# Side matmuls behind PV, the fourth output tile kept in the side bank, an earlier last FFN and a new tile table, in a planned attention + FFN kernel

## The chip, the cores and the metric

One core of a Trainium2 chip. The metric is the device time of one execution in microseconds. A span is shorter than the device time by some 1.8 us: it runs from the first to the last recorded instruction. Three things are called by short names throughout: the **side bank** is PSUM bank 7, the **tail** is what follows the end of the last exponential, **excess** is the time by which an exponential or a tanh ends later after its predecessor than the undisturbed distance of its kind.

## The reference, cut to what matters

```python
x = A_x                                  # 2048 x 512, bf16
xn = layernorm(x)
q = xn @ wq  (32 heads of 16);  k = xn @ wk;  v = xn @ wv      # one K and V for all heads
A = concat_heads(softmax(q k^T / 4) v) @ wo
B = gelu(xn @ w1 + b1) @ w2 + b2         # 512 -> 1792 -> 512, tanh form
return x + A + B
```

## The kernel before

Scores are computed in tiles of 128 keys x 512 queries of one head, 2048 tiles, three to a **unit** (683 units). A unit's three tiles stand in three PSUM banks, and the next unit's in three others. ScalarE takes exp of two or three of them in one instruction. Where the table `DTAB` says `0` or `2`, that tile of the unit goes to VectorE (DVE) instead, which builds an approximate exp from five integer images of the score; PV then takes five matmuls for the tile instead of one. So each such letter takes work from ScalarE (0.427 us, the distance between exponentials of three and of two tiles in the trace) and gives it to DVE (0.68 us for the first piece and a third of 0.548 us for each of the four others) and PE.

```python
# exp(u): ScalarE's share of unit u; the tiles named by DTAB go to p1
exps.append(act(lambda e: e.activation(E[:, s0:s0 + na, :], bank(b0, na)..., ACT.Exp, scale=LN2 / 128.0), ...))
for i, t in enumerate(ts):
    if is_d[t]:
        p1(t, 3 * x + i)                   # DVE reads the score bank
# close_batch: four more images of up to three such tiles, then five PV matmuls for each
```

PE does score matmuls (three side by side in rows of the array), and "column" matmuls of 128x32 weights, four side by side: PV in bank 6, whose sum is called O, and all else, called side matmuls, in the side bank: next queries (`q`), the FFN's first layer (`h`), and the output tiles (`y`: 14 FFN pieces, `wo`: 8 head groups, for each 128 rows). In the trace of the kernel before, the three score matmuls start together and take 0.39 us; the first column matmul starts 0.32 us behind them, and then four start every 0.22 us, each taking 0.38. So the first comes some 0.1 us later than in the rhythm of the fours (an estimate from 0.32 and 0.22). The block of 512 queries is done in 170.75 units; its output tiles are made during the next block, and those of the last block as early as its FFN allows.

The order in each engine's queue is fixed when the kernel is built. The source gives each operation a duration and an `allow`, called its lateness below. A list schedule takes, of what is ready in the plan, the operation with the smallest `rdy + allow`, where `rdy` is the time at which its inputs are ready in the plan (or with the smallest `due`, where one is set). A side operation also has a release: the unit after whose exponential it may be planned at the earliest. The queues run in that order where the chip's durations differ from the plan's too: in the run below that puts side matmuls ahead of PV again, two of DVE's first pieces start only behind an add that stands before them and waits 0.74 us for PE.

```python
return (o.rdy + o.allow if o.due is None else o.due), o.idx         # the key: smallest first

def act(fn, r=(), w=(), n=TBW, allow=0.0, **kw):
    return add("act", fn, r, w, occ=0.051 + n / 1.2e3, lat=0.22, allow=allow, **kw)
def mm4(o, l, rh, start, stop, r=(), w=(), allow=1.5, **ak):        # side matmuls: four columns
    ...
def pv_mm(gg, j, v, kt, rhs, r):
    add("pe", ..., allow=4.0 if gg < NTB * NGR - 1 or kt < NT - 4 else -5.0, kind="pv", tag=(gg, j))

def y_tile(tb, i):                        # last block: FFN part and FIN_G=5 head groups, put by
    y_mm(tb, i, fts=range(FT - FIN_F))
    wo_mm(tb, i, range(FIN_G))
    dve(lambda e: e.tensor_tensor(xpy[:, i, :], pM, x_sb[:, ti, :], ALU.add), ...)     # + residual

FB = (2, 3, 4, 5)                         # the other groups, in score banks that come free at the end
for i in range(4): wo_mm(tb, i, range(FIN_G, NGR - 1), start=True, stop=False, bk=FB[i])
for i in range(4): mm4(bank(FB[i]), oT[last group], wop[:, NGR - 1, :], False, True, ...)
for i in range(4):
    dve(lambda e, i=i, ti=ti: e.tensor_tensor(x_sb[:, ti, :], bank(FB[i]), xpy[:, i, :], ALU.add), ...)
    store(tb, i)
```

Note that PV of the last head group is urgent (-5) only for its last four key tiles; before that a PV matmul (4.0) stands behind a side matmul (1.5) that became ready at the same time.

## Time and profile before

| | before |
|---|---|
| median of 3 runs, before the prediction | 814.35 us (814.28 to 814.74) |
| span of the profiled run, granted clock | 812.5 us, 0.985 |
| busy share of PE, DVE, ScalarE | 96%, 91%, 96% |
| exponentials of three and of two tiles | 265 and 418 |
| end of the last exponential | 799.5 us |
| side matmuls still to do then | 99 by start time |

How to read it: three engines are above 90%, so the shares decide nothing. The chain of waits names ScalarE for 82% of the span; its exponentials stand end to end. What can be won without taking work from ScalarE is the excess between them and the tail. The lines for both stand in the prediction.

### The profile page before, as it was taken

Reading aid. Unit: us, or ns where it says so; the run is one execution under the profiler, and the core shown is the slowest. Engines: PE = TensorE matmul, PEld = TensorE weight load, DVE = VectorE, ACT = ScalarE, POOL = GpSimd, SP = SyncE. Lnnn points to the kernel's source line nnn. Section 1 sums busy time; section 2 is a strip of 40 time slices with the busy share of each in tenths; the row PEclk is TensorE's granted clock in tenths of the full one; section 3 lists DMA queues with packets and bytes.
Section 4 is the critical chain, followed back from the end, with each engine's and each line's share of the span. In section 5 each row is a group of like instructions: output and inputs, shape, how many; then the busy total and the mean of one; then the engine's idle time right before and its main releaser. Section 6 shows DMA issues by size and latency. Waiting matters only on the chain.

```text
span 812.5 us, 21402 instructions
## 1 busy us (share of the span) xinstructions
PE 779.8 (96%) x9184; PEld 240.4 (30%) x9186; DVE 742.5 (91%) x1424; ACT 783.5 (96%) x733; POOL 23.7 (3%) x79
## 2 busy tenths in 40 slices
PE   6799999999999999999999999999999999999998
PEld 4332222222222223222322223322222222322233
DVE  7499999999997898999998769999998898999986
ACT  4899999999999999999999999999999999999993
POOL 6500000000000000000000000000000000000000
PEclk7799999999999999999999999999999999999999
DMA  9000000000000000000000000000000000000000
GB/s 308 13 22 16 16 15 7 23 3 16 15 15 22 28 10 16 15 16 16 15 15 12 19 23 23 15 15 4 16 15 22 22 23 21 10 8 15 16 15 27
DMA packets 23976, 19.09 MB, mean 24 GB/s; under 512 B 12369, under 2 KB 19402, under 8 KB 23882
## 3 DMA queue, kind: packets, MB, share of 16 engines
q1 hardware_dynamic: 22298, 17.17, 7.2%
q8 instruction: 73, 1.20, 0.6%
q10 hardware_dynamic: 1584, 0.56, 0.3%
q14 instruction: 21, 0.17, 0.1%
HBM read 14.98 MB, written 2.35 MB: 21 GB/s over the span
## 4 chain that ended last, share of the span: by engine, by line
ACT 82%; PE 15%; DMA 1%; POOL 1%; DVE 1%; issue 0%; ACTq 0%; POOLq 0%
ACT E L855 78%; PE pAll L551 5%; PE pAll L876 5%; PE pAll L836 4%; ACT ub L978 3%; DMA ub<-in_A_wq_dram 1%; PE pAll L545 1%; ACT ub L675 0%; ACT xnT L693 0%; DVE x_sb L1131 0%; POOL V L794 0%; PE pAll L688 0%; POOL wqp L797 0%; ACT KT L707 0%; ACTq L558 0%
## 5 line engine op out<-in xcount | busy, mean ns | idle before, releaser
L855 ACT ACTIVATE E<-pAll 128x1024 bf16<-128x1024 f32 (+1 forms) x683 | 746.1, 1380 | 3.6 <-PE pAll L836 3.3
L876 PE MATMUL pAll<-Dt,V 128*32 128x512 bf16 x2085 | 349.7, 383 | 0.5
L872 DVE TENSOR_SCALAR Dt<-pAll 128x512 int16<-128x512 f32 x417 | 280.1, 681 | 39.4 <-PE pAll L836 38.4
L876 PE MATMUL pAll<-E,V 128*32 128x512 bf16 x1631 | 301.9, 387 | 1.2 <-DVE Of L900 1.1
L887 DVE TENSOR_SCALAR Dt<-Dt 128x1536 int16<-128x1536 int16 (+2 forms) x600 | 286.1, 519 | 1.0 <-PE pAll L876 0.2
L836 PE MATMUL pAll<-QT,KT 32*128 32x512 bf16 x2048 | 269.1, 387 | 15.5 <-ACT E L855 8.3
L836 PEld LDWEIGHTS pAll<-QT,KT 32*128 32x128 bf16 x2048 | 68.6, 91 | 304.5 <-ACT E L855 247.9
L876 PEld LDWEIGHTS pAll<-Dt,V 128*32 128x32 bf16 x2085 | 94.3, 95 | 87.8 <-issue 45.1
L551 PE MATMUL pAll<-w_sb,ub 128*32 128x512 bf16 x896 | 109.2, 383 | 0.0
L876 PEld LDWEIGHTS pAll<-E,V 128*32 128x32 bf16 x1631 | 73.8, 94 | 61.4 <-issue 44.6
L551 PE MATMUL pAll<-wop,oT 128*32 128x512 bf16 x512 | 81.8, 382 | 0.0
L551 PE MATMUL pAll<-xnT,w_sb 128*32 128x512 bf16 x896 | 80.0, 384 | 1.1 <-DVE hb L964 0.6
L551 PE MATMUL pAll<-xnT,wqp 128*32 128x512 bf16 x496 | 45.1, 398 | 0.5 <-POOL wqp L797 0.3
L1139 PE MATMUL pAll<-xnT,zeros 128*32 128x512 bf16 x396 | 44.1, 384 | 0.0
L964 DVE TENSOR_SCALAR hb<-pAll,b1T 128x512 bf16<-128x512 f32 x56 | 41.2, 735 | 0.0
L551 PEld LDWEIGHTS pAll<-w_sb,ub 128*32 128x32 bf16 x896 | 29.0, 95 | 21.4 <-issue 14.7
L978 ACT ACTIVATE ub<-ub 128x1536 bf16<-128x1536 bf16 (+1 forms) x20 | 31.5, 1576 | 0.0
L730 DVE CAST QT<-pAll 128x512 bf16<-128x512 f32 x32 | 21.7, 680 | 9.8 <-PE pAll L551 7.7
L551 PEld LDWEIGHTS pAll<-xnT,w_sb 128*32 128x32 bf16 x896 | 21.0, 95 | 29.7 <-issue 16.8
L551 PEld LDWEIGHTS pAll<-wop,oT 128*32 128x32 bf16 x512 | 22.3, 95 | 13.6 <-issue 8.5
L900 DVE COPY Of<-pAll 128x512 f32<-128x512 f32 x31 | 21.0, 679 | 0.7 <-PE pAll L876 0.6
L911 DVE TENSOR_TENSOR oT<-Of,rbc 128x512 bf16<-128x512 f32 x31 | 21.1, 679 | 0.0
(109 smaller groups left out, 264.5 us busy)
## 6 DMA issues: line engine op xcount, KB each, us to landing
rbc<-rden_rows SPq DMA_DIRECT2D x124, 64.0 KB, 2.0
w_sb<-in_B_w_dram SPq DMA_DIRECT2D x2, 1792.0 KB, 13.0
x_sb<-in_A_x_dram SPq DMA_DIRECT2D x8, 256.0 KB, 6.9
out_dram<-x_sb SPq DMA_DIRECT2D x16, 128.0 KB, 1.7
QT<-mT SPq DMA_DIRECT2D x60, 2.0 KB
ub<-in_A_wq_dram ACTq DMA_DIRECT2D x1, 512.0 KB, 7.7
wop<-in_A_wo_dram SPq DMA_DIRECT2D x4, 128.0 KB, 2.7
den<-Of SPq DMA_DIRECT2D x31, 8.0 KB
```

Source lines behind the costliest of these rows:

```text
L551: add("pe", lambda e, c=c, j=j: e.matmul(o[c, :], l[:, c], rh, start=start, stop=stop, tile_position=(0, 32 * j)), r, [(k, j) for k in w] ...
L730: dve(lambda e: e.tensor_copy(QT[:, hq, :], bank(bk)), w=[B(bk)] + [(B(bk), j) for j in range(4)] + [("QT", hq)] + [("QTm", hq, j) for j i ...
L836: ins = e.matmul(o, l, rh, start=True, stop=True, tile_position=(q0, 0))
L855: exps.append(act(lambda e: e.activation(E[:, s0:s0 + na, :], bank(b0, na).rearrange("p (a n) -> p a n", a=na), ACT.Exp, scale=LN2 / 128.0 ...
L872: dve(lambda e: e.tensor_scalar(Dt[:, KZ, s, :], bank(bk), float(127 * 128) + SPL_D, SPL_MIN, ALU.add, ALU.max), w=[B(bk), ("D", s, KZ)], ...
L876: add("pe", lambda e, a, b: e.matmul(pO[32 * j:32 * j + 32, :], V1[:, v, kt, :], rhs, start=a, stop=b, tile_position=(0, 32 * j)), r=r + [ ...
L887: dve(lambda e, k=k: e.tensor_scalar(Dt[:, k, s0:s0 + n, :], Dt[:, KZ, s0:s0 + n, :], float(SPL_K[k]), None, ALU.add), r=[("D", s0 + i, KZ ...
L900: dve(lambda e: e.tensor_copy(Of[:, i, :], pO), w=["O", ("Of", i)], allow=0.0)
L911: onorm[gg] = dve(lambda e: e.tensor_tensor(oT[:, gg % NOT, :], Of[:, i, :], rbc[:, i, :], ALU.mult), r=[("Of", i)] + [("rbc", i, j) for j ...
L964: dve(lambda e: e.tensor_scalar(hb[:, ft % 6, :], pM, b1T[:, ft:ft + 1], None, ALU.add), r=["b1T"], w=M4 + [("h", ft % 6)], allow=ev)
L978: act(lambda e: e.activation(uu, uu, ACT.Tanh, scale=GELU_K), r=uk, w=uk, n=c, allow=al - 0.5, kind="tanh")
L1139: pr.filler = lambda e, j, o: e.matmul((pO if o else pM)[32 * j:32 * j + 32, :], zeros[:, 0:32], xnT[:, 0, 0:TBW], start=not o, stop=not o ...
```

## The change

It wants PE's order at the end to put attention first, the tail to lose its DVE adds, and the FFN of the last block to be out of the way earlier; a new table goes with it. The core of the diff (cut: the two tables of 683 letters, new names for values that stay as they were, the plumbing that hands `al` through, and one `due=0.0`, by which the output matmuls of the last head group go to the front of PE's queue once they are ready):

```diff
-LB = 120                       # last block: FFN spread over units LA to LB
-LY = 5                         # output tiles released LY units apart
-LS = 122                       # from unit LS
-FIN_G = 5
+LB = 105
+LY = 9
+LS = 107
+FIN_G = 4
-DTAB = "....2.0202..022.22...2222..."      # 417 tiles on DVE: 124 letters 0, 293 letters 2
+DTAB = "....2.2020.202.2.2...22.2022..."    # 414 tiles on DVE: 148 letters 0, 266 letters 2
+Y_ALLOW = 8.0                  # allow of the output tiles of earlier blocks (was 1.5)
+H_ALLOW = 5.0                  # of the FFN's first layer, earlier blocks alone (was 1.5)
+YT_ALLOW = (3,3,3,3)           # of the last block's output tiles (was 1.5)
+S_LAT = 0.27                   # planned latency of scores (was 0.22)
...
         def y_tile(tb, i):
-            y_mm(tb, i, fts=range(FT - FIN_F))
-            wo_mm(tb, i, range(FIN_G))
-            dve(... xpy = pM + x_sb ...)
+            y_mm(tb, i, al=YT_ALLOW[i])
+            wo_mm(tb, i, range(FIN_G), stop=i < 3, al=YT_ALLOW[i])
+            if i < 3:
+                dve(... xpy = pM + x_sb ...)
+            else:
+                mm4(pM, ident, x_sb[:, ti, :], False, False, ..., allow=YT_ALLOW[i])
...
-        FB = (2, 3, 4, 5)
+        FB = (2, 3, 4, 7)
...
-        for i in range(4):  dve(add of bank FB[i] and xpy); store
+        for i in (0, 1, 3, 2):
+            if i < 3:  dve(add of bank FB[i] and xpy)
+            else:      act(lambda e: e.activation(x_sb[:, ti, :], bank(FB[i]), ACT.Copy))
+            store(tb, i)
```

More of the change, by code (lines that the diff above doesn't have):

```diff
@@ L50 @@
 TBL = 1
-DTAB = "....2.0202..022.22...2222.2022...222.20....002.20.22.202.222....22222.0.020.22.022...2022200...02.0200.0..222..22.000.2202200...2020.2.0.22.0002.2...22222...222.2222.00..2222.2.2022020.202....2.02022.02.22..02....22020..0.222202.0.0..222.2220..22.02020......0..20...22.2222......02200..22.22.2020...2.2222.2.0..22.220...22022.0.0202.222.2...22222.222.20.22220....222020.2.2222.2.2....220.20.0.2202.2......202.2.0..220.0..200.....02..0..222.22.20....222.0.22020.222.0...22.22222.0..2.2220...2.20222..02.22.2020...22222.22.202..2.22...2.22020.22.202.2220..2220.0000.222.22.20...00.22..20.202.02.2....2.0.2.2.2.2.20202...2.20.2.2.2.2.22..20...0202.22.202.02002....22220222.2022.20.20..."
+DTAB = "....2.2020.202.2.2...22.202222..2022.20...2..2..20220.0.2222....2020.20.0202.0.002...2022.200...2.2000.0..220.2.2.0.202002020....002.2.22.0.2002.2...2.222002..02220.02...202.222202.02.2222....022222.202022..222...22200.00.0222.2022...2.20..22.2.2.20.20.....2020..2.22002020....20.22..020.222....0..22.0..2222.0...0220...20.00.0220.2200.22...22222.02.220.22220...2.22020.202202.022....2020.000.2200.2.0....202.2.2..220.0..2.0...0....2.0.2...22.00.....02220.2.222020.0....2.220.20...222222...2.22022.0022.2.2200....2222.22.202..2.22...2.220202.202.2202.0..2220.0000.222.220.....20.22.2200020..02....2..0...22...2.020.0....020202....2.02.20...2022.22.220.02022....22200222.2.2..202.0..."
+Y_ALLOW = 8.0
+H_ALLOW = 5.0
+YT_ALLOW = (3,3,3,3)
+WF_ALLOW = 1.5
+QP_ALLOW = 1.5
+S_LAT = 0.27
+YS = 9
+HA = 40
+HB = 165
 KM_DUE = 5.0
@@ L837, in fn @@
                 return ins
-            return add("pe", fn, r, [B(3 * x + i) for i in range(len(ts))], occ=0.216, lat=0.22, allow=-1.0, kind="S")
+            return add("pe", fn, r, [B(3 * x + i) for i in range(len(ts))], occ=0.216, lat=S_LAT, allow=-1.0, kind="S")
         eptr = [0]
@@ L943, in q_group @@
             for hq in hqs:
-                q_proj(tb, hq, 7, mm4)
+                q_proj(tb, hq, 7, mm4, allow=QP_ALLOW)
                 q_evac(tb, hq, 7, allow=EV_ALLOW)
@@ L962, in h_mm @@
                 mm4(pM, w1_sb[:, d, ft * P:(ft + 1) * P], xnT[:, d, tb * TBW:(tb + 1) * TBW], d == 0, d == DT - 1,
-                   r=["w1"] + tr(4 * tb, 4 * tb + 4), w=[B(7)])
+                   r=["w1"] + tr(4 * tb, 4 * tb + 4), w=[B(7)], allow=H_ALLOW if tb < NTB - 1 else 1.5)
             dve(lambda e: e.tensor_scalar(hb[:, ft % 6, :], pM, b1T[:, ft:ft + 1], None, ALU.add),
@@ L980, in h_chain, with y_mm, wo_mm @@
             dve(lambda e: e.tensor_tensor(uu, uu, hh, ALU.mult), r=uk + hk, w=uk, n=c, mode=2, allow=al)
-        def y_mm(tb, i, start=True, stop=False, bk=7, fts=range(FT)):
+        def y_mm(tb, i, start=True, stop=False, bk=7, fts=range(FT), al=1.5):
             for ft in fts:
                 mm4(bank(bk), ub[:, ft, i * P:(i + 1) * P], w2_sb[:, ft, :], start and ft == fts[0], stop and ft == fts[-1],
-                   r=[("u", ft), "w2"], w=[B(bk)])
-        def wo_mm(tb, i, gs, start=False, stop=True, bk=7):
+                   r=[("u", ft), "w2"], w=[B(bk)], allow=al)
+        def wo_mm(tb, i, gs, start=False, stop=True, bk=7, al=1.5):
             for n, g in enumerate(gs):
@@ L990, in wo_mm @@
                 mm4(bank(bk), oT[:, (tb * NGR + g) % NOT, i * P:(i + 1) * P], wop[:, g, :], start and n == 0,
-                   stop and n == len(gs) - 1, r=[("oT", (tb * NGR + g) % NOT), "wop"], w=[B(bk)])
+                   stop and n == len(gs) - 1, r=[("oT", (tb * NGR + g) % NOT), "wop"], w=[B(bk)], allow=al)
         def store(tb, i):
@@ L997, in out_tile @@
         def out_tile(tb, i):
-            y_mm(tb, i)
-            wo_mm(tb, i, range(NGR))
+            y_mm(tb, i, al=Y_ALLOW)
+            wo_mm(tb, i, range(NGR), al=Y_ALLOW)
             ti = tb * 4 + i
@@ L1006, in y_tile @@
         def y_tile(tb, i):
-            y_mm(tb, i, fts=range(FT - FIN_F))
-            wo_mm(tb, i, range(FIN_G))
             ti = tb * 4 + i
-            dve(lambda e: e.tensor_tensor(xpy[:, i, :], pM, x_sb[:, ti, :], ALU.add), r=[("x", ti)],
-                w=M4 + [("x", 2 * i), ("x", 2 * i + 1)], allow=EV_ALLOW)
+            y_mm(tb, i, al=YT_ALLOW[i])
+            wo_mm(tb, i, range(FIN_G), stop=i < 3, al=YT_ALLOW[i])
+            if i < 3:
+                dve(lambda e: e.tensor_tensor(xpy[:, i, :], pM, x_sb[:, ti, :], ALU.add), r=[("x", ti)],
+                    w=M4 + [("x", 2 * i), ("x", 2 * i + 1)], allow=EV_ALLOW)
+            else:
+                mm4(pM, ident, x_sb[:, ti, :], False, False, r=["ident", ("x", ti)], w=[B(7)], allow=YT_ALLOW[i])
         UPT = NU / NTB
@@ L1037, in bass_parallel_sum__grouped_kv_mqa__dense_activation_gelu__prompt_kernel @@
                 for i in range(4):
-                    at(u0 + 3 + 9 * i, lambda tb=tb, i=i: out_tile(tb - 1, i), 0.6)
+                    at(u0 + 3 + (YS if tb < NTB - 1 else 9) * i, lambda tb=tb, i=i: out_tile(tb - 1, i), 0.6)
                 q_pair(tb, (6, 7), u0 + 50)
-            a, b = (40, 165) if tb < NTB - 1 else (LA, LB)
+            a, b = (HA, HB) if tb < NTB - 1 else (LA, LB)
             if tb == 0:
@@ L1119, in bass_parallel_sum__grouped_kv_mqa__dense_activation_gelu__prompt_kernel @@
         tb = NTB - 1
-        FB = (2, 3, 4, 5)
+        FB = (2, 3, 4, 7)
         for i in range(4):
-            wo_mm(tb, i, range(FIN_G, NGR - 1), start=True, stop=False, bk=FB[i])
-        for i in range(4):
-            if FIN_F:
-                y_mm(tb, i, start=False, bk=FB[i], fts=range(FT - FIN_F, FT))
+            wo_mm(tb, i, range(FIN_G, NGR - 1), start=i < 3, stop=False, bk=FB[i], al=WF_ALLOW)
         for i in range(4):
             mm4(bank(FB[i]), oT[:, (NTB * NGR - 1) % NOT, i * P:(i + 1) * P], wop[:, NGR - 1, :], False, True,
-               r=[("oT", (NTB * NGR - 1) % NOT) if i < 2 else ("oTl", 1), "wop"], w=[B(FB[i])])
-        for i in range(4):
+               r=[("oT", (NTB * NGR - 1) % NOT) if i < 2 else ("oTl", 1), "wop"], w=[B(FB[i])], due=0.0)
+        for i in (0, 1, 3, 2):
             ti = tb * 4 + i
-            dve(lambda e, i=i, ti=ti: e.tensor_tensor(x_sb[:, ti, :], bank(FB[i]), xpy[:, i, :], ALU.add),
-                r=[("x", 2 * i), ("x", 2 * i + 1)], w=[(B(FB[i]), j) for j in range(4)] + [B(FB[i]), ("x", ti)])
+            w = [(B(FB[i]), j) for j in range(4)] + ([B(FB[i])] if i < 3 else []) + [("x", ti)]
+            if i < 3:
+                dve(lambda e, i=i, ti=ti: e.tensor_tensor(x_sb[:, ti, :], bank(FB[i]), xpy[:, i, :], ALU.add),
+                    r=[("x", 2 * i), ("x", 2 * i + 1)], w=w)
+            else:
+                act(lambda e, i=i, ti=ti: e.activation(x_sb[:, ti, :], bank(FB[i]), ACT.Copy), w=w)
             store(tb, i)
```

## The prediction

> **What bounds the kernel now.** I first read the chain that ended last, because busy shares alone cannot say which of three engines above 90% (PE 96%, DVE 91%, ACT 96%) sets the time:
>
> ```profile
> ACT 82%; PE 15%; DMA 1%; POOL 1%; DVE 1%; issue 0%; ACTq 0%; POOLq 0%
> ```
>
> ScalarE's row of exponentials is the chain for four fifths of the span. Next, ScalarE's own groups with shapes kept apart (line, shapes, count, busy us, mean ns, idle before and what ended it):
>
> ```profile
> L855 ACT ACTIVATE E<-pAll 128x1024 bf16<-128x1024 f32 x418 | 434.8, 1217 | 2.9 <-PE pAll L836 2.6 <-PE pAll L876 0.2
> L855 ACT ACTIVATE E<-pAll 128x1536 bf16<-128x1536 f32 x265 | 401.6, 1636 | 0.8 <-PE pAll L836 0.7
> ```
>
> The 683 exponentials waited 3.7 us in all. Their recorded durations overlap, so I took the distance from one end to the next, whose middle values are steady: 0.9165 us for two tiles, 1.3435 us for three. The 20 tanh's take 1.3615 (16) and 0.935 (4). Then 418 x 0.9165 + 265 x 1.3435 + 25.5 = 764.6 us of ScalarE work that nothing in this change shortens. From the first exponential's end (32.1 us) to the last's (799.5 us) there are 767.4; leaving the first exponential out of the work, the excess summed step by step is 4.1 us. ScalarE's row in order of time shows where it lies:
>
> ```profile
> 39.93 1.94 ACT L855 ACTIVATE E<-pAll 128x1024 bf16<-128x1024 f32 x2 [0.24 <-PE pAll L836]
> 42.93 54.96 ACT L855 ACTIVATE E<-pAll 128x1024 bf16<-128x1024 f32 x51 [1.07 <-PE pAll L836]
> ...
> 661.34 43.11 ACT L855 ACTIVATE E<-pAll 128x1024 bf16<-128x1024 f32 x39 [0.58 <-PE pAll L836]
> ...
> 786.10 1.94 ACT L855 ACTIVATE E<-pAll 128x1024 bf16<-128x1024 f32 x2 [0.49 <-PE pAll L836]
> 788.29 11.22 ACT L855 ACTIVATE E<-pAll 128x1024 bf16<-128x1024 f32 x10 [0.26 <-PE pAll L836]
> ```
>
> Split: 1.9 us before 43 us (the granted clock is at half from 28.6 to 42.3 us in the trace), 0.3 at 302, 0.7 at 661, 1.2 after 786. So the span is a head of 30.6 us, a ScalarE stretch with 4 us of slack in it, and a tail of 812.5 - 799.5 = 13.0 us. Only slack and tail can be won.
>
> The tail, from the order of time on PE and DVE:
>
> ```profile
> 802.52 0.88 DVE L918 COPY Of<-pAll 128x256 f32<-128x256 f32 x2 [3.50 <-PE pAll L876]
> 803.92 0.21 DVE L924 RECIPROCAL rT<-pAll 128x8 f32<-128x8 f32 x1 [0.52 <-PE pAll L545]
> ...
> 806.20 0.42 DVE L939 TENSOR_TENSOR oT<-Of,pAll 128x256 bf16<-128x256 f32 x1 [0.27 <-PE pAll L935]
> 807.05 1.88 DVE L1131 TENSOR_TENSOR x_sb<-pAll,x_sb 128x512 bf16<-128x512 f32 x3 [0.44 <-PE pAll L551]
> ...
> 808.86 0.68 DVE L1010 TENSOR_TENSOR x_sb<-pAll,x_sb 128x512 f32<-128x512 f32 x1
> 809.57 0.69 DVE L1131 TENSOR_TENSOR x_sb<-pAll,x_sb 128x512 bf16<-128x512 f32 x1
> ```
>
> Three pieces: 3.0 us from the last exponential to the first copy of O (DVE idle 3.5 us for PV), 4.5 us of normalisation to the first final add, and 5.4 us of five DVE adds and the store. What PE did after 799.5 us (groups of PE in that window):
>
> ```profile
> L551 PE MATMUL pAll<-wop,oT 128*32 128x512 bf16 x67 | 7.5, 380 | 0.0
> L551 PE MATMUL pAll<-w_sb,ub 128*32 128x512 bf16 x38 | 5.8, 380 | 0.0
> L876 PE MATMUL pAll<-Dt,V 128*32 128x512 bf16 x5 | 1.7, 379 | 0.0
> ...
> L876 PE MATMUL pAll<-E,V 128*32 128x512 bf16 x2 | 0.4, 379 | 0.0
> ```
>
> Only 7 PV matmuls were left, but 105 side matmuls shared their queue; the DVE pieces that feed the last PV were finished by 799.01, yet its matmuls start as late as 801.89 and 802.10. That is an order, not a dependence. The end is also in the last output tile's FFN part, whose add (L1010) runs at 808.86, between the final adds.
>
> [...] four column matmuls start per 0.21 to 0.22 us, and the first of a visit follows the score matmuls by 0.32. [...] The trace: (1343.5 - 916.5) / 512 = 0.834, so one more tile on ScalarE costs 0.427 us. [...]
>
> **The change part by part.**
>
> *New table.* I counted its letters: 269 dots for 266, of which the last is the two-tile remainder. So there are 268 three-tile and 415 two-tile exponentials: 3 x (1.3435 - 0.9165) = +1.3 us on ScalarE, on the path. DVE loses three tiles, at 0.68 + 4 x 0.18 = 1.4 us each (0.68 for the first piece, a third of 0.548 us for each of four others): -4.2 us, mostly beside ScalarE. PV falls from 3716 to 2070 + 1634 = 3704 matmuls. In the last quarter the table has 102 such tiles where it had 107, so late DVE and PE are relieved more (5 x 1.4 = 7 us of DVE, 20 PV matmuls).
>
> *FFN and output tiles earlier.* The last block's FFN ends 15 units sooner, and its output tiles are released at units 107, 116, 125, 134 of the block instead of 122, 127, 132, 137. At the 1.16 us per unit measured from 661 to 799.5 us, the first is released 17 us earlier. The four need 4 x 4 x 18 + 4 = 292 small matmuls (14 FFN pieces, 4 head groups; 4 for the identity). Room: from 612.2 to 658.0 us, 43 units, PE did 224 PV and 252 side matmuls, or 11 per unit. PV takes 224 / 43 = 5.2 of them, so 5.8 are left at best. Before, the release at unit 122 of 170.75 left 48.75 units for 304 matmuls (19 pieces), and 38 + (67 - 48) = 57 of them fell past the last exponential (48 of the 67 are the last groups' own): so 247 / 48.75 = 5.1 places a unit were really had. From unit 107, 63.75 units give 5.1 x 63.75 = 325 for 292. The fit is narrow: the earlier FFN competes with the previous block's output tiles for the same bank.
>
> *Side behind PV.* Its cost is nil in instructions. It should remove most of the 3.0 us: [...] I take 1.1. Saved: 1.9 us. In the slack it should help late (1.2 after 786) and at 661, where bursts of side matmuls delay scores; I take 1.4 of 2.2 us.
>
> *Fourth tile in the side bank.* Removes one L1010 (0.68 us) from the tail and moves one final add from DVE to ScalarE, idle then: its copy of a rescaled 128x256 costs 0.41 us without a table load, its 128x512 evacuation from PSUM (L707) 0.69. Final adds fall from 5 to 3 on DVE: 1.9 us instead of 3.2, so 1.3 saved. The store after the last add stays 2.2 us (810.26 to 812.5). PE gains four identity matmuls (0.2 us, before the end), and of the head groups that wait for score banks there are now 36 matmuls (3 tiles, 3 groups) where there were 32; at four per 0.213 us that is 1.9 us, and the normalisation leaves PE about 1.8 (4.55 less 1.05 and 0.88 of its own matmuls and 0.85 for the last group). Their cost on the path: 0.1.
>
> Sum: +1.3 (table) - 1.4 (slack) - 1.9 (PV) - 1.3 (adds) + 0.1 = -3.2 us. 814.35 - 3.2 = 811.15; I say 811.2.
>
> **Rivals.** *The tail does not shrink because PE is full:* the bank-7 chain of FFN, previous outputs and four output tiles is serial, and PE has only some 33 places to spare. Then side matmuls again run past the last exponential, now behind PV, and delay only the fourth tile. For: before, tiles finished 16 us apart, and the last at 808.86. Against: 17 us earlier release. Result 812.5 to 813.5. *Deferral costs scores or buffers:* side matmuls pushed back 8 us hold the side bank, FFN pieces come late, DVE bunches them before the pieces that free score banks. For: DVE 91% busy. Against: DVE waited 38.4 us for scores and DVE has 4.2 us less to do. Result 814 to 817. *The slack vanishes altogether, head included:* another order under the half clock saves part of the 1.9. Against: the head of the table hardly differs, the score ring has only two halves. Result 809 to 810. *Table only:* if the tail was bound by something the new order leaves, +1.3 stays, 815.6; against it is DVE's 3.5 us wait for PV itself.
>
> **Range and chances.** A floor is 764.6 + 1.3 + head 30.6 + a tail of 9.2 + 1.85 (measured time less span) = 807.6 with no stall, less or more a few tenths for the overlap at the seams. A gain over 2% means under 798, below that floor, so 0.01. A loss over 2% needs 16 us of new stalls in a schedule with 4; 0.01. 809.3 covers a tail near its best with less slack; 814.0 covers the first rival and a little of the second.
>
> **What would show it.** Right: exponentials 415 and 268, first piece x414; excess on ScalarE near 2.7, its last end within 0.5 of 799.5; first copy of O 0.8 to 1.4 us after it; no L1010-like add after it; three final DVE adds with a ScalarE copy beside them; tail 9.4 to 10.2. Wrong: PE side matmuls of the FFN still running past the last exponential, or excess of 5 us or more in the middle, or the half clock granted again after 43 us.

Behind the -1.9, a derivation counted 0.2 us from ScalarE to PE and 0.2 from PE to DVE, and got "0.8 us at best" for the copy of O. The trace of the kernel before has PE's weight load 0.05 us after the last exponential's end (at 799.57 us), PV matmuls of 0.38 us, and DVE's copy 0.04 us after the modelled end of the last one. What is left for the room on PE is the counts: 11 column matmuls per unit, 5.2 of them PV.

## More of the kernel before

One more view answers why the last block's FFN comes late: busy time by engine for 700 to 759 us of the kernel before (window, its length, then busy us and count of PE, PE's weight loads, DVE, ScalarE, GpSimd, the granted clock, DMA).

```profile
700.00:759.00 59.00, 55.72 (x634) 17.15 (x630) 58.02 (x105) 59.00 (x53) 0.00 (x0) 1.00 0.05 12
```

DVE is busy 58.0 of 59.0 us there, and the last gelu, a chain of five DVE operations and a tanh, ends at 759.8 us. The first output tile can be finished only then: 48 of its 56 FFN matmuls start from 747.8 us on, the last eight at 760.1.

## The result, and the profile after

The changed kernel took 810.53 us (median of 4 runs, 810.0 to 811.37), the kernel before 814.32 (4 runs, 813.75 to 814.74). The ratio is 0.9955, 95% interval 0.9938 to 0.9972. Ratios here are the mean time of one kernel's fast runs over that of the other's fast runs of the same rounds, so not quite the ratio of the medians.

The chain of the kernel after, its exponentials (line numbers moved by 9), and what ScalarE waited for in order of time (start us, length us, engine, line, operation, output<-input, shapes, count, and in brackets the idle time before and its releaser):

```profile
ACT 81%; PE 17%; DMA 1%; POOL 1%; issue 0%; DVE 0%; ACTq 0%; POOLq 0%
```

```profile
L864 ACT ACTIVATE E<-pAll 128x1024 bf16<-128x1024 f32 x415 | 428.1, 1194 | 0.9 <-PE pAll L845 0.8
L864 ACT ACTIVATE E<-pAll 128x1536 bf16<-128x1536 f32 x268 | 401.0, 1613 | 1.8 <-PE pAll L845 1.5
```

```profile
256.53 76.02 ACT L864 ACTIVATE E<-pAll 128x1024 bf16<-128x1024 f32 x70 [0.23 <-PE pAll L845]
333.40 10.49 ACT L864 ACTIVATE E<-pAll 128x1536 bf16<-128x1536 f32 x9 [0.85 <-PE pAll L845]
...
448.34 4.20 ACT L864 ACTIVATE E<-pAll 128x1024 bf16<-128x1024 f32 x4 [0.57 <-PE pAll L845]
```

The counts are as the table's letters say. But the waits have moved: none is left after 786 us, and three are new in the middle. The tail of the kernel after, from the order of time:

```profile
800.06 0.88 DVE L927 COPY Of<-pAll 128x256 f32<-128x256 f32 x2 [2.68 <-PE pAll L885]
...
803.71 0.42 DVE L948 TENSOR_TENSOR oT<-Of,pAll 128x256 bf16<-128x256 f32 x1 [0.28 <-PE pAll L944]
...
804.13 2.14 DVE L1142 TENSOR_TENSOR x_sb<-pAll,x_sb 128x512 bf16<-128x512 f32 x3
...
806.19 0.60 ACT L1145 ACTIVATE x_sb<-pAll 128x512 bf16<-128x512 f32 x1 [3.65 <-PE pAll L560]
```

The last exponential ends at 799.54; O is copied 0.5 us later, the first final add starts at 804.13, and the end is ScalarE's copy, which waited 3.65 us for PE. What PE did after 799.5 us:

```profile
L560 PE MATMUL pAll<-wop,oT 128*32 128x512 bf16 x73 | 5.5, 381 | 0.0
L560 PE MATMUL pAll<-x_sb,ident 128*32 128x512 bf16 x4 | 1.3, 379 | 0.0
...
L560 PE MATMUL pAll<-w_sb,ub 128*32 128x512 bf16 x3 | 1.0, 386 | 0.0
```

Almost no FFN pieces are left; by start time there are 73 side matmuls behind the last exponential, where there were 99 (the prediction's group view counts 105: the view takes what overlaps the window). Counted as the prediction does, without the last head groups' own (48 before, 64 after, as `FIN_G` fell from 5 to 4), what is left over fell from 51 to 9, four of them the identity matmuls. And the same 59 us window as above:

```profile
700.00:759.00 59.00, 57.81 (x682) 18.32 (x678) 56.72 (x101) 59.00 (x52) 0.00 (x0) 1.00 0.04 11
```

DVE has 1.3 us more room, and the last gelu ends at 752.9 instead of 759.8 us; PE runs 682 matmuls instead of 634. Counted from the end of unit 602's exponential to that of unit 645's, the column matmuls rose from 432 to 481, of which PV fell from 224 to 204 and `y` and `wo` rose from 48 to 109. That is where the work was done that used to lie behind the last exponential.

The last block's first layer, however, does not begin earlier. In both kernels it begins just after the previous block's fourth output tile has left the side bank (680.0 and 687.0 us), so 7 us later than before. Its first matmuls, before and after:

```profile
680.43 0.61 PE L551 MATMUL pAll<-xnT,w_sb 128*32 128x512 bf16 x8
687.40 0.62 PE L560 MATMUL pAll<-xnT,w_sb 128*32 128x512 bf16 x8
```

So all that is won lies within the FFN's own stretch, 79.3 us from this matmul to the last gelu's end before and 65.5 after.

The whole span, part by part. ScalarE's work is counts times the undisturbed distances of the prediction, and the excess is split at 60 and at 750 us. The last column is a later run of the same kernel, explained below.

| us | before | after | after, again |
|---|---|---|---|
| end of the first exponential | 32.1 | 31.8 | 31.4 |
| ScalarE's own work from there | 763.3 | 764.6 | 764.6 |
| excess: head, middle, late | 1.9, 1.0, 1.2 | 0.9, 2.3, 0.0 | 2.2, 2.3, 0.0 |
| tail: to the copy of O | 3.0 | 0.5 | 0.5 |
| tail: copy of O to first final add | 4.5 | 4.1 | 4.1 |
| tail: from there to the end | 5.4 | 5.1 | 5.0 |
| span | 812.5 | 809.2 | 810.1 |

### The profile page after: what moved, and what is told of

Same layout as the page of the kernel before. It is cut to its first block, busy times and chain, and to the rows that moved or that the text cites. A ratio compares the mean times of both kernels' runs of the same rounds, so it can differ in the third digit from the quotient of the medians.

```text
span 809.2 us, 21055 instructions
## 1 busy us (share of the span) xinstructions
PE 782.9 (97%) x9082; PEld 245.4 (30%) x9082; DVE 739.7 (91%) x1403; ACT 785.3 (97%) x734; POOL 23.7 (3%) x79
## 4 chain that ended last, share of the span: by engine, by line
ACT 81%; PE 17%; DMA 1%; POOL 1%; issue 0%; DVE 0%; ACTq 0%; POOLq 0%
ACT E L864 77%; PE pAll L885 7%; PE pAll L845 5%; PE pAll L560 4%; ACT ub L987 3%; DMA ub<-in_A_wq_dram 1%; PE pAll L554 1%; ACT ub L684 0%; ACT xnT L702 0%; POOL V L803 0%; PE pAll L697 0%; POOL wqp L806 0%; ACT KT L716 0%; PE pAll L1152 0%; ACTq L567 0%
## 5 line engine op out<-in xcount | busy, mean ns | idle before, releaser
L885 PE MATMUL pAll<-Dt,V 128*32 128x512 bf16 x2070 | 362.7, 383 | 0.3 <-DVE Dt L896 0.2
L881 DVE TENSOR_SCALAR Dt<-pAll 128x512 int16<-128x512 f32 x414 | 278.4, 683 | 33.9 <-PE pAll L845 33.0
L885 PE MATMUL pAll<-E,V 128*32 128x512 bf16 x1634 | 297.1, 389 | 1.1 <-DVE Of L909 0.9
L885 PEld LDWEIGHTS pAll<-Dt,V 128*32 128x32 bf16 x2070 | 99.1, 94 | 103.3 <-issue 50.8
L560 PE MATMUL pAll<-w_sb,ub 128*32 128x512 bf16 x896 | 115.3, 382 | 0.0
L560 PE MATMUL pAll<-xnT,w_sb 128*32 128x512 bf16 x896 | 109.5, 382 | 0.2
L885 PEld LDWEIGHTS pAll<-E,V 128*32 128x32 bf16 x1634 | 70.3, 93 | 80.8 <-issue 64.8
L560 PE MATMUL pAll<-wop,oT 128*32 128x512 bf16 x512 | 87.8, 381 | 0.0
L560 PE MATMUL pAll<-xnT,wqp 128*32 128x512 bf16 x496 | 39.6, 391 | 0.8 <-DVE QT L739 0.4
L560 PEld LDWEIGHTS pAll<-xnT,w_sb 128*32 128x32 bf16 x896 | 29.5, 95 | 21.1 <-issue 7.5
L1152 PE MATMUL pAll<-xnT,zeros 128*32 128x512 bf16 x300 | 31.0, 383 | 0.0
```

Of the source, the lines that this page charges most:

```text
L560: add("pe", lambda e, c=c, j=j: e.matmul(o[c, :], l[:, c], rh, start=start, stop=stop, tile_position=(0, 32 * j)), r, [(k, j) for k in w] ...
L881: dve(lambda e: e.tensor_scalar(Dt[:, KZ, s, :], bank(bk), float(127 * 128) + SPL_D, SPL_MIN, ALU.add, ALU.max), w=[B(bk), ("D", s, KZ)], ...
L885: add("pe", lambda e, a, b: e.matmul(pO[32 * j:32 * j + 32, :], V1[:, v, kt, :], rhs, start=a, stop=b, tile_position=(0, 32 * j)), r=r + [ ...
L1152: pr.filler = lambda e, j, o: e.matmul((pO if o else pM)[32 * j:32 * j + 32, :], zeros[:, 0:32], xnT[:, 0, 0:TBW], start=not o, stop=not o ...
```

## The experiments

All were correct against the reference but `y2_pv_first_less`, which is meant to be wrong (its error stayed within the tolerance, so it counted as correct too). A time is always set beside the kernel before on the same chip.

### The changed kernel again: how much of the gain is the change?

No edit.

> The changed kernel once more, as the measure for the others of this batch. Theory A (the gain is the tail: 13.0 to 9.7 us, and the table's +1.3 is paid by 1.0 less stall in the head and 1.2 less late): 810 to 811.4 us, last exponential ending at 799.5 if the half clock lasts to 38.9 us as in its first profile, about 1 us later if it lasts to 42.3 us as in the kernel before. Rival H (the head's 1 us belongs to the change and not to where the clock's windows fall): the half clock ends at 38.9 us in every profile of it.

Measured: 811.54 us (5 runs, 810.61 to 812.14), before 813.54 (11 runs, 812.0 to 814.67), ratio 0.9976 (0.9963 to 0.9988). Theory A (the median 0.1 above its range), and against H: in this profile the half clock lasts to 41.7 us, and the head's waits are those of the kernel before. ScalarE in order of time from 38 to 50 us, in this run:

```profile
39.27 2.11 ACT L864 ACTIVATE E<-pAll 128x1024 bf16<-128x1024 f32 x2 [0.24 <-PE pAll L845]
42.34 8.95 ACT L864 ACTIVATE E<-pAll 128x1024 bf16<-128x1024 f32 x8 [0.96 <-PE pAll L845]
```

and in the first profile of the same program, where the half clock ended at 38.9 us, one uninterrupted row:

```profile
37.04 13.27 ACT L864 ACTIVATE E<-pAll 128x1536 bf16<-128x1536 f32 x12
```

The same queue, instruction for instruction, waits 1.0 us at 42.3 us in one run and not at all in the other. This half-clock stretch lasts 13.7 us in this profile and in that of the kernel before, and 10.2 us in the first profile of the changed kernel, 3.4 less; what sets its length is not shown. In the kernel before, a score matmul takes 0.60 us at the half clock (32 to 42 us) and 0.38 from there on. Between the two profiles of the changed kernel the longer stretch goes with 1.3 us more of waits in the head (2.2 against 0.9). So runs have to be compared at like granted clock. The five runs of before at 0.984 and 0.985 average 814.34 us, and the two of after at 0.985 and 0.987 average 811.98: 2.4 less. At 0.989 it is 813.35 (two) against 811.14 (two): 2.2 less. At 0.992 it is 812.38 (four runs) against 810.61 (one): 1.8 less. The change is worth about 2 us. Of the 3.8 first seen, part of the rest can be unequal clock: the changed kernel's runs had 0.987 to 0.991 there, but of the kernel before only the profiled run's clock, 0.985, is on record, so this is not shown.

### The old table on the new order

```diff
-DTAB = (new)
+DTAB = (old)
```

> The changed kernel with the table of before. Theory A: 418 and 265 exponentials again, so 1.3 us less ScalarE work, which the time shows only if the stalls stay; tail within 0.5 of 9.7; time 809 to 811. Rival T (the new table is what keeps the late stretch without stalls and PE free at the end): late excess back to 1 us or more, copy of O later than 1 us after the last exponential, time 812 or more.

Measured: 837.65 us (6 runs), ratio 1.029 (1.0262 to 1.0318). Theory A fails and T has the sign right (its third mark, a copy of O more than 1 us after the last exponential, is missed narrowly with 0.95), but neither expected 26 us more than the changed kernel took. The last exponential ends at 813.7 us with 12.1 us of excess in the middle and 4.9 late, and the tail is 25.1 us, because the output tiles are far behind. PE's groups after the last exponential:

```profile
L560 PE MATMUL pAll<-w_sb,ub 128*32 128x512 bf16 x188 | 11.6, 380 | 2.6 <-DVE x_sb L1020 2.6
L560 PE MATMUL pAll<-wop,oT 128*32 128x512 bf16 x119 | 8.8, 379 | 0.0
```

Three tiles more on DVE do not weigh that much by themselves. The build plans every queue from the table, so with another table nearly every decision falls otherwise. The trace also has the clock at half in five stretches between 118 and 770 us, 20.5 us in all, where the changed kernel has none after 43 us; how much of the 26 us is a slower PE and how much the order was not separated. This run says nothing about what the letters cost; it says that a table is fitted to its order.

### Side matmuls ahead of PV again

```diff
-Y_ALLOW = 8.0;  H_ALLOW = 5.0;  YT_ALLOW = (3,3,3,3)
+Y_ALLOW = 1.5;  H_ALLOW = 1.5;  YT_ALLOW = (1.5,1.5,1.5,1.5)
```

> The changed kernel with all the new lateness allowances of side matmuls set back to 1.5, so that they stand before PV again. Theory A: PV is late again at the end, the copy of O starts 1.5 to 3 us after the last exponential instead of 0.5, tail 11 to 12.5, time 812 to 813.5. Rival E (it is the earlier release that emptied PE's queue, not the order): copy of O stays within 0.5 us of where it was, time within 0.5 us of the changed kernel.

Measured: 824.67 us (4 runs), ratio 1.0137. Theory A misses its mechanism: O is copied 0.51 us after the last exponential and the tail is 9.7 us, as with the new latenesses. E has the tail right and the time wrong: of the 14.0 us between this profile's span and that of the changed kernel, 12.6 are excess in the middle (14.9 against 2.3 us) and 1.5 late. Two stretches of half clock, at 475 and 598 us, lie in it, and waits of 1.4 and 1.3 us follow them, at 478 and 603 us. One such wait, in order of time, shows how it comes about:

```profile
253.31 1.90 PE L560 MATMUL pAll<-wop,oT 128*32 128x512 bf16 x29
...
255.25 0.69 DVE L1010 TENSOR_TENSOR x_sb<-pAll,x_sb 128x512 bf16<-128x512 f32 x1 [0.74 <-PE pAll L885]
...
255.86 1.28 DVE L881 TENSOR_SCALAR Dt<-pAll 128x512 int16<-128x512 f32 x2
...
257.12 3.77 ACT L864 ACTIVATE E<-pAll 128x1024 bf16<-128x1024 f32 x4 [2.38 <-PE pAll L845]
```

PE runs a burst of 29 `wo` matmuls until 255.2. DVE's add of that output tile stands in its queue ahead of the next first pieces (L881); DVE waits for the burst although the view names PV, which overlaps it. Only when the first of those pieces has ended, at 256.5, do the scores come: they start at 256.69, and ScalarE has stood for 2.4 us. So on this table the latenesses keep waits off the exponentials, in the middle and late. For the tail this run says little, since 14 us of waits give PE time to catch up (66 side matmuls are left); the run with the last four tiles alone, below, bears on it.

### The fourth output tile in its own score bank again

```diff
-FB = (2, 3, 4, 7)         # tile 3: residual by PE's identity matmul, copy by ScalarE
+FB = (2, 3, 4, 5)         # tile 3 as the others: DVE adds the residual, then a fourth final add
```

> The changed kernel with the fourth output tile handled as the other three: evacuated from the side bank with the residual by DVE, last groups in a fourth score bank, four final adds on DVE. Theory A: the fourth tile's matmuls still fall behind the last exponential, so its L1010-like add lands among the final adds: five DVE adds, first add to last add 3.2 us instead of 2.1 (2.7 with ScalarE's copy); tail 10.2 to 11, time 0.4 to 1.2 us above the changed kernel. Rival P (PE sets the end there, adds are hidden): within 0.3 us of it.

Measured: 812.9 us (5 runs), ratio to before 0.9994, so 1.4 us above the changed kernel by medians, a little over theory A's 0.4 to 1.2. The mean spans differ by 1.1 us (810.7 and 809.6): in this run device time exceeds the span by 1.9 to 2.7 us, which no trace explains. The middle is the same to the hundredth (excess 2.29), which makes this a clean comparison: the tail is 10.44 us instead of 9.56. Theory A, 0.9 us. Five DVE adds run from 5.03 to 8.24 us after the last exponential; the fourth tile's own add stands between the final ones:

```profile
807.25 0.68 DVE L1020 TENSOR_TENSOR x_sb<-pAll,x_sb 128x512 f32<-128x512 f32 x1
```

### The new table alone

```diff
 (kernel before)
-DTAB = (old)
+DTAB = (new)
```

> The kernel before with the new table alone. Theory F (a table and an order of PE's queue fit only each other, because the order decides when score banks and buffers come free; the old table on the new order cost 26 us): stalls all over the middle, 10 us or more of them, time 824 to 838. Rival N (the old order takes any table of the same size; only the late side matmuls of the new order are touchy): middle stalls below 3 us, time 814.5 to 816 (1.3 us more ScalarE work).

Measured: 831.02 us (4 runs), ratio 1.0219; excess 20.6 us in the middle and 2.6 late. Theory F. Yet O is copied 0.51 us after the last exponential and 53 side matmuls are left: with waits all through, PE has time to keep up. Here too the clock is at half in three stretches (349, 359 and 598 us, 10.2 us in all), with waits of 1.4 and 1.6 us soon after, at 363 and 605 us.

### The earlier release alone

```diff
 (kernel before)
-LB = 120;  LY = 5;  LS = 122
+LB = 105;  LY = 9;  LS = 107
```

> The kernel before with nothing but the earlier end of the last FFN and the earlier release of its output tiles (units 105 and 107, 9 apart). Theory R (the release empties PE's queue at the end): copy of O starts 0.5 to 1.2 us after the last exponential instead of 3.0, middle as before, tail 10.5 to 12, time 1 to 2.5 us below the kernel before. Rival O (PV must also stand before the side matmuls): copy of O later than 2 us, time within 0.7 us of before.

Measured: 812.93 us (4 runs, before 813.29), ratio 0.9994 (0.9979 to 1.0009). Theory R fails outright. 99 side matmuls are left, the tail is 12.98 us, and the copy of O has the wait of the kernel before:

```profile
801.55 0.88 DVE L918 COPY Of<-pAll 128x256 f32<-128x256 f32 x2 [3.50 <-PE pAll L876]
```

The release was not what held the FFN back on the old table: the last gelu ends at 758.8 us of a run that began its exponentials 0.9 us sooner. The edit hardly reached the program: only 14 of the 1424 places in DVE's order differ from the kernel before, and none in ScalarE's. That DVE has no room to take the FFN earlier is the likely reason, but argued from its 58.0 busy us of 59.0.

### The last four tiles alone ahead of PV

```diff
-YT_ALLOW = (3,3,3,3)
+YT_ALLOW = (1.5,1.5,1.5,1.5)
```

> The changed kernel with the lateness of the last block's four output tiles alone set back from 3 to 1.5; the middle is untouched. Theory R: copy of O within 0.3 us of 0.52 after the last exponential, time within 0.8 us of the changed kernel. Rival O: copy of O 1.5 us or more after it, time 1 us or more above the changed kernel.

Measured: 813.1 us (4 runs), ratio 0.9995. O is copied at 0.51 us, as R said; the time is above R's limit and is O's. The first final add now comes at 6.43 instead of 4.59 us after the last exponential, and the tail is 11.02 us, 1.4 to 1.5 more. 85 side matmuls are left instead of 73. The final adds wait for PE, where in the changed kernel they did not:

```profile
806.70 1.89 DVE L1142 TENSOR_TENSOR x_sb<-pAll,x_sb 128x512 bf16<-128x512 f32 x3 [1.85 <-PE pAll L560]
```

This profile also has a half-clock stretch at 341 us, with 1.0 us of excess at 348. Neither theory is right about why: PV is in time, and the tail is longer nonetheless. That turned the question from PV to the amount that PE has left.

### The late release on the new order

```diff
-LB = 105;  LY = 9;  LS = 107
+LB = 120;  LY = 5;  LS = 122
```

> The changed kernel with the last FFN and output tiles released as late as before (units 120 and 122, 5 apart), the new lateness kept. Theory R: more than 100 side matmuls after the last exponential where the changed kernel has 73, and the copy of O 1.5 us or more after it. Rival O: copy of O stays at 0.5 to 0.8, since PV goes first, and the whole backlog falls on the fourth tile: its copy on ScalarE ends 9 us or more after the last exponential (7.24 now). Either way 1.5 us or more above the changed kernel, some of it from new stalls that the shifted FFN brings.

Measured: 818.55 us (4 runs), ratio 1.0064. The head and middle are those of the changed kernel (excess 4.65 us), and O is copied at 0.52 us, as O said; 163 side matmuls are left, as R said. They fall on the third and, most of all, the fourth tile:

```profile
808.64 3.21 PE L560 MATMUL pAll<-w_sb,ub 128*32 128x512 bf16 x56 [0.78 <-DVE x_sb L1020]
...
813.91 0.60 ACT L1145 ACTIVATE x_sb<-pAll 128x512 bf16<-128x512 f32 x1 [10.54 <-PE pAll L560]
```

ScalarE's copy waits 10.5 us for PE, and the tail is 16.3 us. With the new order and table the earlier release is needed: it is worth 6.8 us of tail there, and nothing on the old pair.

### PV first at the end, alone

```diff
 (kernel before)
-allow=4.0 if gg < NTB * NGR - 1 or kt < NT - 4 else -5.0
+allow=4.0 if gg < NTB * NGR - 1 or kt < NT - 8 else -5.0
```

> The kernel before with one number changed: PV matmuls of the last eight key tiles instead of the last four are urgent, so that no side matmul stands before the last PV; table, releases and everything to the last exponential as before. Theory W (PE's leftover work sets the tail: what goes behind PV has to be done all the same, before the fourth tile's end): copy of O at 0.5 to 0.8 us after the last exponential instead of 3.0, but the tail stays within 0.5 us of 12.95 and the time within 0.5 us of before. Theory O (the late PV held up the chain by its 2.5 us): tail 10.3 to 11, time 1.8 to 2.6 us below before.

Measured: 812.55 us (4 runs, before 812.9), ratio 0.999 (0.9972 to 1.0008). Theory W. The last exponential ends at 799.12 us, and the tail in DVE's order of time is:

```profile
799.63 0.88 DVE L918 COPY Of<-pAll 128x256 f32<-128x256 f32 x2
...
805.23 1.89 DVE L1131 TENSOR_TENSOR x_sb<-pAll,x_sb 128x512 bf16<-128x512 f32 x3 [1.51 <-PE pAll L551]
808.19 0.69 DVE L1010 TENSOR_TENSOR x_sb<-pAll,x_sb 128x512 f32<-128x512 f32 x1 [1.08 <-PE pAll L551]
```

O is copied 2.5 us sooner, and it helps by 0.25: the tail is 12.70 us. Side matmuls that were passed over (120 are left, where there were 99) now hold up the final adds, in two waits of 1.5 and 1.1 us.

### The same with less left for PE

```diff
 (kernel of the run before this)
-y_mm(tb, i, fts=range(FT - FIN_F))
+y_mm(tb, i, fts=range(FT - FIN_F - (7 if i == 3 else 0)))     # wrong on purpose
```

> The same, with 28 of the fourth output tile's 76 side matmuls left out (seven of fourteen FFN pieces; its result is wrong on purpose), so that PE's backlog at the last exponential is about that of the changed kernel. Theory W: tail 1.2 to 2.0 us shorter than in the run with PV first alone, 28 matmuls at 0.053 us each. Theory O: the same tail as that run.

Measured: 812.32 us (4 runs), ratio 0.9988; the profile's tail is 11.53 us, 1.17 less, just under W's range, for 28 matmuls less (92 left). The last wait is gone and the first is not:

```profile
805.52 1.89 DVE L1131 TENSOR_TENSOR x_sb<-pAll,x_sb 128x512 bf16<-128x512 f32 x3 [1.51 <-PE pAll L551]
807.32 0.68 DVE L1010 TENSOR_TENSOR x_sb<-pAll,x_sb 128x512 f32<-128x512 f32 x1
```

The medians differ by only 0.2 us, within their spread, so the verdict rests on the profile's tail; the head's excess of this profile was 0.6 us larger, which hides half of it.

### PV first and the side bank, on the old table

```diff
 (kernel before)  NT - 4 -> NT - 8, the fourth tile and due=0.0 as in the change
```

> PV first as above and the fourth tile kept in the side bank with PE's residual and ScalarE's copy, on the kernel before, with its table and releases. Theory W: 0.3 to 1.2 us below the run with PV first alone (own bank cost 0.9 on the changed kernel, but PE carries four matmuls more here and is full), time 811.5 to 813.2 on a chip where before takes 813.3. Theory O: all of the tail's gain and none of the table's 1.3 us: tail 9.7 to 10.3, time 810 or less, better than the changed kernel.

Measured: 812.48 us (4 runs), ratio 0.9991; tail 12.09 us, 0.6 less than with PV first alone. Theory W by the tail; by medians the two runs differ by 0.07 us only, less than W's 0.3. 124 side matmuls are left. The first final add comes at 4.60 us after the last exponential, as in the changed kernel, instead of 6.11 (`due=0.0` would do that; it was not tested alone); in its place ScalarE's copy waits 6.3 us for PE. The parts of the change that concern the tail's form do little while PE is behind.

### Order and table fitted again

The plan counts an exponential as 0.051 us + n / 1.2e3. The distances of the trace, 0.9165 us for 1024 elements and 0.000834 for each, give 0.9165 - 1024 x 0.000834 = 0.063 us for the first term; over 683 exponentials the difference is 8 us. I put 0.063 in, and let a search change letters, releases and latenesses. It judged each candidate by a replay of the planned queues with the durations of the traces, an estimate.

```diff
-occ=0.051 + n / 1.2e3
+occ=0.063 + n / 1.2e3
-DTAB = (new, 414 tiles on DVE)
+DTAB = (another, 429 tiles on DVE)
-LA, LB, LY, LS, FIN_G = 34, 105, 9, 107, 4
+LA, LB, LY, LS, FIN_G = 29, 114, 12, 122, 5
-Y_ALLOW, H_ALLOW, YT_ALLOW, WF_ALLOW, QP_ALLOW = 8, 5, (3,3,3,3), 1.5, 1.5
+Y_ALLOW, H_ALLOW, YT_ALLOW, WF_ALLOW, QP_ALLOW = 4, 4, (2,7,-2,4), -4.5, 2.5
-YS, HA, HB = 9, 40, 165
+YS, HA, HB = -1, 42, 164
```

> The changed kernel with its order planned from ScalarE's measured 63 ns of fixed cost for an exponential instead of 51, and table, releases and latenesses fitted again to that plan and to a replay of the queues with the measured durations: 429 tiles on DVE instead of 414. Theory F (order and table have to be fitted together, and what bounds the time is ScalarE's own work as long as the fit holds): 15 x 0.427 = 6.4 us less ScalarE work than the changed kernel, excess stalls 3 to 5 us, tail 9.8 to 10.6; last exponential near 792, time 802.5 to 806. Rival D (DVE, at 91%, and PE cannot carry 15 more tiles; waits replace the work saved): excess above 8 us, or tail above 13, time 808 or more. With the profile goes the number of half-clock windows after 43 us[...].

The cost of a half-clock stretch: the waits soon after such stretches in the runs above were 1.0, 1.3, 1.4, 1.4 and 1.6 us.

Measured: 806.63 us (6 runs, 804.13 to 807.45), before 813.3 (11 runs, 811.39 to 814.37), ratio 0.9923 (0.9912 to 0.9935). It beats both kernels; the median is 0.6 us above the range of F, the profiled run inside it. Its profile:

```profile
PE 39%; DVE 32%; ACT 26%; POOL 1%; issue 1%; DMA 1%; ACTq 0%; POOLq 0%; DVEq 0%
```

```profile
L864 ACT ACTIVATE E<-pAll 128x1024 bf16<-128x1024 f32 x430 | 433.9, 1126 | 0.3 <-PE pAll L845 0.2
L864 ACT ACTIVATE E<-pAll 128x1536 bf16<-128x1536 f32 x253 | 375.5, 1552 | 1.1 <-PE pAll L845 0.6 <-PE pAll L885 0.3
```

The last exponential ends at 792.24 us with 3.2 us of excess in all, the tail is 10.2 us. The chain that ended last now runs through PE and DVE more than through ScalarE, so the three queues are near balance. ScalarE still has only these 3.2 us of waits, and 6.4 of the 7.7 us by which this span is shorter than the changed kernel's second one are work taken off it. The run changes table, order, releases and the planned cost together; what each is worth was not separated. The profiled run was the fastest of the six, with a granted clock of 0.991 where the others have 0.985 to 0.987; so the typical run has some 2.5 us more than this profile shows.

## Why the prediction was right or wrong

The time, 811.2 with a range of 809.3 to 814.0, was right (810.53), and so was the bound: ScalarE's work and its tail. That the sum of -3.2 us came so near the measured -3.8 is in part luck, since at like clock the change is worth about 2 us and several steps were off in both directions.

- **New table, +1.3 us on ScalarE: right.** 268 and 415 exponentials; work 763.3 to 764.6 us.
- **Slack, -1.4 us: right in part, and partly by luck.** Late waits went from 1.2 to 0.0 us as foreseen, and came back with 1.5 us when the latenesses were undone. The middle did not lose its waits but went from 1.0 to 2.3 us. The head fell by 1.0 us in the first profile and rose by 0.3 in the second of the same program. At an equal clock in the head the slack is not won at all: 4.1 us before, 4.5 in the second profile.
- **Side behind PV, -1.9 us: the size was near, the reason wrong.** The step said that the late PV was "an order, not a dependence", which PV first alone confirms (the copy of O comes at 0.51 instead of 3.00 us), and that its removal shortens the tail by its wait, which is the part that failed. The wait shrank by 2.5 us, even more than said; but the order alone took only 0.25 us off the tail (12.70 against 12.95), since PE's passed-over work came due at the final adds. What shortened the tail, beside the fourth tile's 0.9 us below, is less work left: 73 side matmuls instead of 99. With O copied 0.5 us after the last exponential in every case, the tail is 11.5 us with 92 left, 12.7 with 120 and 16.3 with 163 (other things differ too between these kernels; only the step from 120 to 92 is a test of the amount alone). How the rest is ordered counts as well: with the last four tiles back at 1.5 the tail is 11.0 us. Nor is it shown that the latenesses made PV timely: the copy comes at 0.51 to 0.52 us in every run with the changed kernel's table, whichever other part was undone (in two of these runs waits also gave PE time); with the old table it comes at 3.00, with the new order on it at 0.95, and at 0.51 where PV was made urgent.
- **FFN and output tiles earlier: right that the fit is narrow, wrong on what opens it.** The first tile was done 7.4 us sooner (755.5 against 762.9 us), where the step released it 17 us sooner. I took the release as the gate. It is one on the new order (6.8 us of tail), but on the old pair the release alone changed nothing. That DVE, 58.0 of 59.0 us busy, was the gate, and that the new table's five fewer tiles in the last quarter opened it, is argued from the windows and the gelu's end; a table cannot be changed alone without changing every queue, so this is not shown. The side bank may be a second gate, as the step foresaw: in both kernels the FFN begins just after the previous block's outputs have left it.
- **Fourth tile in the side bank, -1.3 us: over by half.** Undone on the changed kernel it costs 0.9 us; on the old table, with PE behind, 0.6. The adds on DVE fell from five to three as said, but PE's identity matmuls, held to cost nothing before the end, were issued at 802.0 to 804.7, after the last exponential, and ScalarE's copy waited 3.65 us for PE. From the first final add to the end it took 5.1 us instead of the 4.1 that the step implied.
- **Rivals.** The first, side matmuls that run past the last exponential and then delay the fourth tile alone, is in the trace: ScalarE's wait of 3.65 us. It came together with the main line instead of in its place. The second, new waits in the middle, is there with 1.3 us; whether deferral causes just these three was not tested, and taking the deferral away made the middle worse by 12.6 us. The third, all slack gone, did not come (3.2 and 4.5 us of excess); nor did the table-only one (815.6).
- **Signs.** Counts, the last exponential's end (799.54 in the first profile), the adds and the tail (9.65 and 9.56) came as listed; the copy of O was earlier than 0.8 us. Of the signs of being wrong one came in small: two FFN matmuls still started behind the last exponential.

In sum, at equal clocks: +1.3 for the table, +1.3 in the middle, -1.2 late, +0.3 in the head, -3.4 in the tail, so -1.7 us by the profiles of before and of the second run (whose span is shorter by another 0.7, as its first exponential came sooner on that chip), and -2.0 by that call's ratio (0.0024 x 813.5). What else the first measurement's 3.8 us holds stays open; unequal clock can be part of it.

## What to carry to other kernels

When a queue runs in program order, as here, moving one kind of work ahead of another shortens the end only if what was passed over has somewhere else to go (here PV first alone brought the copy of O 2.5 us forward and the end only 0.25): count what the engine has left when its feeder stops, and shorten that. A fixed order, the durations that it was planned with and the split of work between engines are one fit: judge changes to them by fitting again (here 806.6 us), since each half with the other's partner came out 18 and 24 us above the kernel before. And before a difference of 1 us is explained, look at where the half-clock stretches lie in both profiles (here one 3.4 us longer went with 1.3 us more of waits).
